# Routed attention with an ELU layer: row sums of two blocks in one set of matmuls, spread by GpSimd's transfers, and the first keys cut at 512

## The chip, the cores and the metric

The kernel runs on one core of one Trainium2 chip. The metric is device microseconds of one launch, the median of the runs shown. TensorE's granted clock is full in this execution (0.999 mean), so times of the two kernels can be compared line by line.

## The reference, cut to what matters

There are 4 batches (b), 8 heads, 768 tokens, head dimension 64 and 16 clusters; everything is fp32. A query may look at a key only where both are nearest to the same centroid of their head:

```
q_assign, k_assign = argmax over the 16 centroids of q_n . c_n and k_n . c_n
scores = q k^T / 8, and -1e9 where q_assign != k_assign
attn   = exp(scores - max); attn = attn / (sum(attn) + 1e-9)
x      = attn v                  # laid out as 3072 tokens x 512
out    = elu(x w_in) w_out       # w_in 512 x 2048, w_out 2048 x 512
```

## The kernel before

**Layout.** Scores are made transposed: keys on partitions, queries in the free dimension. One *block* is a batch, a half of the queries (`HS` = 384) and a pair of heads, so there are 32 blocks, 8 to a batch, counted n = 0 to 31. `at` = n mod 8 is the place in the batch. Keys come in six tiles of 128 (`kt`). The two heads of a pair are called e = 0 and 1.

**A slot** (`slot(n)`, about 10 us) is written out by hand (`manual_schedule`): every engine runs its instructions in the order of the text, and waits come from the data alone. On TensorE a slot is

- `row_sums(n - 2)` (L554): two matmuls of 64 ones by the 384 partial sums of head 0 and of head 1. They give the denominator of each query, already repeated on the 64 partitions of its head, in the PSUM bank `d_bank`;
- `values(n - 1)` (L536): twelve matmuls, probabilities times v, into `o_bank`;
- in the slots with `at` = 5, 6, 7 and one early slot of each batch (3 in the first, 1 later), `similar` (L427): four matmuls with 32 columns each, cluster scores for later queries or keys, into `d_bank`;
- six times `plain` (L498, q k^T) and `masked` (L511, adds the mask from one-hot cluster rows), into three banks used in turn (`ring`).

ScalarE runs `take_sums` (L563 Ln of the row sums, L564 a copy with its sum over the row, L565 Exp, together a first reciprocal), then `take_values` (L550, `o_bank` to `xT`), six exponentials (L520, into `p_out`), and the deferred list `later`, emptied by `flush` at the end of the slot: the copies of the one-hot rows (L456), the mask step for GpSimd (L463) and the conversion step of the weights (L330).

VectorE runs `sums_end` (L528 and L529: the six probability tiles added up, from 768 x 6 to 768), `divide` (L568, L569: one Newton step on the reciprocal), `assign` where the slot has one (L440, L442, L443, L453: the argmax), transposes of the next q and k (L659, L666, L673), the *weight steps* that `weigh` has planned, and `sums_begin` (L523). `divide` ends with one multiplication on GpSimd (L572) that scales the block of `xT`.

**Weight steps.** The weights arrive as 64-bit words and are turned to fp32 by `begin` (L320, L328 on VectorE, then L330 on ScalarE) and three `join`s (L340, L344, L350). `ROOM` gives each slot a credit, so what runs in which slot is fixed when the kernel is built.

**The start** (`slot_first`). The first q and k are turned by TensorE (`turned`, L577, copied out by ScalarE at L594) rather than VectorE, in halves of 384 keys: four pairs of heads, cluster scores of the first 384 keys, then the second half likewise. `assign` runs for the first q, the first and the second half of k. Then come the first six `plain`, `masked` and exponentials.

**After the attention** come the two matrix products with Strassen-like splits (L748, L994, L1066), fed by `w_step`, `elu_exp` and `elu`. The row sums of blocks 30 and 31 are done just ahead of the first product and inside its first unit (`finish_attention`). `findings` checks the row sums and the cluster counts on the chip; a general path runs only if that check fails.

**Buffers that the change names.** `summed`, `r_of`, `e_of` and `add_to` are parts of `sums_w`; `spare` holds weight words and later the products' temporaries. SyncE's queue issues nearly all transfers; GpSimd's own queue issues twelve stores of weight sums (L732) and two additions (L1390).

Of the kernel before, what the change touches and what calls it, by code (L numbers as in the profile page):

```python
# [19 lines left out]
P = 128  # L20
# [41 lines left out]
def main_path(ctx, tc, c, q, k, v, centroids, moe_w_in, moe_w_out, out):  # L62
# [71 lines left out]
    top = early[:, 7488:7512]  # L134
    hot_q = early[:, 7512:7896].bitcast(BF16).rearrange("p (s n) -> p s n", s=2)
# [3 lines left out]
    summed = sums_w[:, 4 * HS : 6 * HS]  # L139
# [111 lines left out]
    cT = const.tile([P, P], F32, name="cT")  # L251
    count = const.tile([P, 4 * B], F32, name="count")
    counted = 0
    r_sum = const.tile([P, len(blocks)], F32, name="r_sum")
    d_sum = const.tile([P, len(blocks)], F32, name="d_sum")
# [54 lines left out]
    def begin():  # L310

        nonlocal split
        if not wide:
            split += 1
            ask()
            return
        ask()
        w = words[split][0]
        to, e = like(pieces[split][0], w), like(ex_of, w)
        nc.vector.tensor_scalar(  # L320
            to.bitcast(U32),
            w[:, :, :, 1],
            0xFFFFF,
            1 << 20,
            op0=Alu.bitwise_and,
            op1=Alu.bitwise_or,
        )
        nc.vector.tensor_scalar(e, w[:, :, :, 1], 0x7FF00000, None, op0=Alu.bitwise_and)  # L328
        split += 1
        later.append(lambda: nc.scalar.activation(e, e, Act.Relu, scale=8.0, bias=off))  # L330
# [63 lines left out]
    credit, later = 0.0, []  # L394

    def flush():
        for other in later:
            other()
        later.clear()
# [25 lines left out]
    def similar(t, cols, ps):  # L425
        for pr in range(NPR):
            nc.tensor.matmul(  # L427
                ps[32 * pr : 32 * pr + 32, :HS],
                lhsT=cT[:, 32 * pr : 32 * pr + 32],
                rhs=t[pr][:, cols],  # L430
                start=True,
                stop=True,
            )

    def assign(hot, ps):


        nonlocal counted
        n = HS // NC
        nc.vector.transpose(sim, ps[:, :HS])  # L440
        s = sim.rearrange("p (n c) -> p n c", c=NC)
        nc.vector.tensor_reduce(top, s, axis=Axis.X, op=Alu.max)  # L442
        nc.vector.scalar_tensor_tensor(  # L443
            oh.rearrange("p (n c) -> p n c", c=NC),
            s,
            1.0,
            top.unsqueeze(2).to_broadcast([P, n, NC]),
            op0=Alu.mult,
            op1=Alu.is_equal,
            accum_out=count[:, counted : counted + 1],  # L450
        )
        counted += 1
        nc.vector.transpose(hot[:, 0], oh)  # L453
        for e in range(2):
            later.append(
                lambda e=e: nc.scalar.copy(  # L456
                    hot[64 * (1 - e) : 64 * (1 - e) + 64, 1], hot[64 * e : 64 * e + 64, 0]
                )
            )
# [12 lines left out]
    def clusters_k(b, half, ps):  # L472
        cols = ts(half, HS)
        similar(kT[b % 2], cols, ps)
        return lambda: assign(hot_k[b % 2][:, :, cols], ps)
# [11 lines left out]
    turn_of = 0  # L487
# [39 lines left out]
    def sums_end():  # L527
        nc.vector.tensor_tensor(add_to, add_to, probs_all[:, 8 * HS :], op=Alu.add)  # L528
        nc.vector.tensor_tensor(  # L529
            summed, add_to[:, : 2 * HS], add_to[:, 2 * HS :], op=Alu.add  # L530
# [21 lines left out]
    def row_sums(n):  # L552
        for e in range(2):
            nc.tensor.matmul(  # L554
                d_bank[64 * e : 64 * e + 64, :HS],
                lhsT=ones,
                rhs=summed[:, ts(e, HS)],
                start=True,
                stop=True,
            )  # L560

    def take_sums(n):
        nc.scalar.activation(r_of, d_bank[:, :HS], Act.Ln)  # L563
        nc.scalar.activation(e_of, d_bank[:, :HS], Act.Copy, accum_out=d_sum[:, n : n + 1])  # L564
        nc.scalar.activation(r_of, r_of, Act.Exp, scale=-1.0)  # L565

    def divide(n):
        nc.vector.tensor_tensor(e_of, e_of, r_of, op=Alu.mult)  # L568
        nc.vector.scalar_tensor_tensor(  # L569
            r_of, e_of, -2.0, r_of, op0=Alu.add, op1=Alu.mult, accum_out=r_sum[:, n : n + 1]  # L570
        )
        nc.gpsimd.tensor_tensor(x_of(n), x_of(n), r_of, op=Alu.mult)  # L572
# [8 lines left out]
    def turn(to, t, n):  # L581

        for i in range(HT):
            turned_by_pe(to[:, ts(i, P)], t, n + i)

    turns = 0

    def turned(to, t, n):
# [4 lines left out]
        turn(bank, t, n)  # L593
        nc.scalar.copy(to, bank[:, :HS])  # L594

    def slot_first():
# [10 lines left out]
        for pr in range(NPR):  # L607
            turned(kT[0][pr][:, :HS], first_k[pr], 0)
        told = [clusters_k(0, 0, o_bank)]
        flush()  # L610
        for pr in range(NPR):
            turned(kT[0][pr][:, HS:], first_k[pr], HT)
# [8 lines left out]
        for kt in range(NT):  # L621
            s = ring()
            plain(0, kt, s)
# [8 lines left out]
    def slot(n):  # L632
        b, at = n // NB, n % NB
        more = b + 1 < B
        if n > 1:
            row_sums(n - 2)
            take_sums(n - 2)
# [9 lines left out]
        if n > 0:  # L647
            sums_end()
        if n > 1:
            divide(n - 2)  # L650
# [24 lines left out]
        weigh(n)  # L675

# [7 lines left out]
        flush()  # L684
# [678 lines left out]
    def findings():  # L1363
# [6 lines left out]
        nc.vector.tensor_scalar(ok[:, 1:2], peak[:, 1:2], D_MAX, None, op0=Alu.is_lt)  # L1370
        nc.vector.tensor_scalar(same, count, float(HS // NC), None, op0=Alu.is_equal)
# [10 lines left out]
    last_n = len(blocks) - 1  # L1382
# [14 lines left out]
    row_sums(last_n - 1)  # L1397
    values(last_n)
    sums_end()
# [3 lines left out]
    take_sums(last_n - 1)  # L1403
    divide(last_n - 1)
    take_values(last_n)

    def finish_attention():
        row_sums(last_n)
        take_sums(last_n)
        divide(last_n)  # L1410
# [21 lines left out]
    for u in range(4):  # L1432
# [3 lines left out]
        if u == 1:  # L1436
            findings()
# [278 lines left out]
```

## Time and profile before

| what | value |
|---|---|
| median of 3 runs | 902.42 us (902.07 to 902.99) |
| the profiled execution: its time, its span | 902.24 us, 900.5 us |
| TensorE matmul busy | 889.9 us |
| VectorE busy | 725.9 us; 48.5 of each 50 us in the attention from 100 to 300 us |
| ScalarE, GpSimd busy | 449.5 us, 226.0 us |
| attention (to the first product at 341.6 us) | 38% of the span |
| row sums L554 | 32 times two matmuls, each of them two records: x128, 27.7 us busy |
| `divide` L568, L569 | 551 and 595 ns, x32 each |
| `take_sums` L563, L564, L565 | 480, 481 and 519 ns, x32 each |

Busy times are unions: matmuls in different columns of the array run at once, so 128 records of 512 ns make 27.7 us. A record's end is modelled, so distances in this document are taken from start to start.

### The profile page before, as it was taken

The page shows a single profiled execution, that of the slowest core. Times are in us where ns is not written, and L with a number is a line of the kernel's source. Part 1 is how long each engine was busy: PE and PEld are TensorE (multiplying, and loading weights), DVE is VectorE, ACT ScalarE, POOL GpSimd, SP SyncE. Part 2 cuts the span into 40 slices and gives each one's busy share as a digit, 9 for nine tenths or more (in the row PEclk, how much of TensorE's full clock was granted, in tenths as well). Part 3 has the DMA queues.
Part 4 walks back from the last instruction along what each step waited for, and adds up shares of the span by engine and source line. Part 5 has one row for each costly group of instructions (what it writes and reads, how often), then busy time and mean ns, then how long its engine had stood idle before and what let it go on. Part 6 is the DMA issues. An engine that isn't in the chain of part 4 may idle for free.

```text
span 900.5 us, 17050 instructions
## 1 busy us (share of the span) xinstructions
PE 889.9 (99%) x6473; PEld 687.6 (76%) x6473; DVE 725.9 (81%) x1067; ACT 449.5 (50%) x883; POOL 226.0 (25%) x257
## 2 busy tenths in 40 slices
PE   8999999999999999999999999999999999999997
PEld 4444444444444447899989999999999999999997
DVE  4699999999999997995389965895589558956885
ACT  5677787777776774420133225522552255225421
POOL 1022031221303244870033002520252025202300
PEclk9999999999999999999999999999999999999999
DMA  6765554365323622102698766176717761767272
GB/s 197 195 110 137 153 137 80 105 135 139 71 82 96 192 88 71 70 13 95 199 296 302 241 206 220 50 242 206 218 55 241 212 210 58 240 210 209 58 221 87
DMA packets 153209, 138.33 MB, mean 154 GB/s; under 512 B 89248, under 2 KB 106656, under 8 KB 152096
## 3 DMA queue, kind: packets, MB, share of 16 engines
q1 hardware_dynamic: 151584, 132.45, 50.2%
q0 software_dynamic: 1248, 4.20, 1.5%
q8 instruction: 53, 0.87, 0.4%
q10 hardware_dynamic: 288, 0.52, 0.2%
q14 instruction: 36, 0.29, 0.1%
HBM read 114.59 MB, written 21.50 MB: 151 GB/s over the span
## 4 chain that ended last, share of the span: by engine, by line
PE 92%; DVE 4%; DMA 2%; SPq 1%; issue 0%; ACT 0%; DVEq 0%
PE bank L994 23%; PE bank L748 16%; PE banks L498 12%; PE o_bank L536 12%; PE bank L1066 9%; PE o_bank L994 4%; PE o_bank L748 3%; PE banks L511 3%; PE d_bank L994 2%; PE d_bank L554 2%; PE o_bank L1066 2%; PE d_bank L427 1%; SPq L166 1%; DMA w_out<-in_k_dram 1%; PE d_bank L1066 1%; PE d_bank L748 1%
## 5 line engine op out<-in xcount | busy, mean ns | idle before, releaser
L520 ACT ACTIVATE p_out<-banks 128x768 f32<-128x768 f32 x192 | 155.2, 811 | 26.8 <-PE banks L511 25.4
L536 PE MATMUL o_bank<-p_out,kq_g 128*64 128x384 f32 x768 | 129.4, 486 | 0.1
L536 PEld LDWEIGHTS o_bank<-p_out,kq_g 128*64 128x64 f32 x768 | 55.0, 137 | 69.2 <-issue 62.7
L762 POOL TENSOR_SCALAR kq_g<-kq_g 128x512 f32<-128x512 f32 x96 | 67.8, 715 | 152.0 <-ACT kq_g L761 151.6
L572 POOL TENSOR_TENSOR xT<-xT,sums_w 128x384 f32<-128x384 f32 x32 | 35.3, 1103 | 222.0 <-DVE sums_w L569 164.6
L523 DVE TENSOR_TENSOR sums_w<-p_out 128x1536 f32<-128x1536 f32 x32 | 57.1, 1785 | 7.5 <-ACT p_out L520 7.5
L994 PE MATMUL bank<-w_out,kq_g 128*128 128x128 f32 x512 | 63.1, 275 | 0.0
L528 DVE TENSOR_TENSOR sums_w<-sums_w,p_out 128x1536 f32<-128x1536 f32 x32 | 59.0, 1845 | 3.3 <-DVE sums_w L523 0.5
L994 PEld LDWEIGHTS bank<-w_out,kq_g 128*128 128x128 f32 x512 | 60.5, 192 | 0.5
L761 ACT ACTIVATE kq_g<-bank 128x512 f32<-128x512 f32 x68 | 39.8, 602 | 38.9 <-PE bank L748 17.3
L748 PE MATMUL bank<-xT,spare 128*128 128x256 f32 x256 | 59.2, 379 | 0.0
L748 PEld LDWEIGHTS bank<-xT,spare 128*128 128x128 f32 x256 | 48.3, 190 | 6.4
L748 PE MATMUL bank<-x_sum,w_in 128*128 128x256 f32 x224 | 52.9, 379 | 0.0
L765 DVE SCALAR_TENSOR_TENSOR kq_g<-kq_g,bank 128x512 f32<-128x512 f32 x68 | 44.9, 680 | 6.2 <-POOL kq_g L762 6.2
L748 PEld LDWEIGHTS bank<-x_sum,w_in 128*128 128x128 f32 x224 | 42.6, 190 | 5.8
L1280 DVE TENSOR_TENSOR kq_g<-kq_g 128x1024 f32<-128x1024 f32 x36 | 45.2, 1263 | 1.5 <-PE bank L994 1.5
L1084 POOL TENSOR_TENSOR spare<-x_sum 128x128 f32<-128x128 f32 x16 | 7.3, 455 | 154.4 <-PE bank L1066 88.8
L463 POOL TENSOR_SCALAR kq_g<-w_out,big,minus 128x768 bf16<-128x768 bf16 x16 | 34.1, 2138 | 46.8 <-ACT w_out L456 46.8
L550 ACT ACTIVATE xT<-o_bank 128x384 f32<-128x384 f32 x32 | 15.7, 490 | 48.3 <-PE o_bank L536 48.3
L498 PE MATMUL banks<-x_sum,xT 64*128 64x384 f32 x192 | 39.8, 492 | 0.0
L498 PE MATMUL banks<-x_sum,kq_g 64*128 64x384 f32 x192 | 39.6, 491 | 0.0
L498 PE MATMUL banks<-kq_g 64*128 64x384 f32 x192 | 39.6, 491 | 0.0
(326 smaller groups left out, 2030.2 us busy)
## 6 DMA issues: line engine op xcount, KB each, us to landing
kq_g<-in_v_dram SPq DMA_DIRECT2D x32, 384.0 KB, 3.6
sums_w<-far_s_s SPq DMA_DIRECT2D x42, 256.0 KB, 3.7
spare<-w_far SPq DMA_DIRECT2D x32, 256.0 KB, 3.1
words_w<-far_s_s SPq DMA_DIRECT2D x26, 256.0 KB, 3.5
out_dram<-p_out SPq DMA_DIRECT2D x22, 256.0 KB, 3.4
w_out<-in_q_dram SPq DMA_DIRECT2D x112, 48.0 KB, 2.7
sums_w<-far_s_q SPq DMA_DIRECT2D x21, 256.0 KB, 3.6
words_w<-far_a_s SPq DMA_DIRECT2D x20, 256.0 KB, 3.7
```

What stands on the lines that cost most here:

```text
L498: nc.tensor.matmul(s[:, e, :HS], lhsT=kT[b % 2][pr][rows, ts(kt, P)], rhs=qT[half][pr][rows], start=True, stop=False,)
L520: nc.scalar.activation(probs[kt], s[:, :, :HS], Act.Exp, scale=SCALE)
L523: nc.vector.tensor_tensor(add_to, probs_all[:, : 4 * HS], probs_all[:, 4 * HS : 8 * HS], op=Alu.add)
L528: nc.vector.tensor_tensor(add_to, add_to, probs_all[:, 8 * HS :], op=Alu.add)
L536: nc.tensor.matmul(o_bank[64 * e : 64 * e + 64, :HS], lhsT=v_raw[n % 2][:, e, kt], rhs=probs[kt][:, e], start=(kt == 0), stop=(kt == NT - 1),)
L748: nc.tensor.matmul(bank[:, ts(f, QS)], lhsT=left[:, ch, ts(f, P)], rhs=right[:, ch], start=first and f == 0 and ch == 0, stop=ch == 1, ski ...
L761: nc.scalar.activation(to, as_part(bank, to), Act.Exp)
L762: nc.gpsimd.tensor_scalar(to, to, 1.0, 0.0, op0=Alu.min, op1=Alu.max)
L765: nc.vector.scalar_tensor_tensor(to, to, -1.0, as_part(bank, to), op0=Alu.add, op1=Alu.max)
L994: nc.tensor.matmul(bank[:, :P], lhsT=left[:, f], rhs=right[:, f], start=first and f == 0, stop=last and f == 3, skip_group_check=True,)
L1066: nc.tensor.matmul(bank[:, ts(f, P)], lhsT=left[:, ts(f, P)], rhs=right, start=m in ("m1", "m5") and f == 0, stop=True, skip_group_check=True,
L1280: nc.vector.tensor_tensor(b[to][:, f], b[x][:, f], b[y][:, f], op=op)
```

## The change

1. **Row sums.** They are done in odd slots only, for the two blocks n - 3 and n - 2 at once. Four matmuls of 32 ones (`ones[:, :32]`) fill the four 32-row strips of `d_bank`: block n - 3 head 0, head 1, block n - 2 head 0, head 1. The last two blocks follow in the first unit of the product. `summed` becomes two buffers; the new one lies in `spare`.
2. **Their reciprocals.** `take_sums` and the Newton step run once for a pair of blocks, on 128 partitions. `reciprocals` goes to a place in `xT` (or `add_to`) that is not yet in use. It comes behind the weight steps on VectorE; before, `divide` stood ahead of `assign`, the transposes and the weight steps.
3. **The spread.** Each sum now stands on 32 partitions where 64 are wanted. Two transfers issued by GpSimd copy 64 rows twice each into `r_of` and `e_of` (128 x 384 fp32, 192 KB each). In the next slot `scale_x` multiplies the two blocks on GpSimd.
4. **ScalarE's conversion step** L330 goes on a list of its own (`powers`), emptied in the next slot behind `take_sums`; before, it was ahead of it.
5. **The first k** is cut in 512 and 256 keys. Pair 0's last 256 are turned ahead of the cluster scores of the first part, and the first `plain` goes ahead of the second cluster scores. The counts that `findings` compares are corrected for the sizes.

```diff
+    CUT = 512
+    told_in = {
+        HS: (sim, oh, top),
+        CUT: (p_out[:, :512], p_out[:, 512:768].bitcast(BF16), p_out[:, 768:800]),
+        S - CUT: (sim[:, :256], oh[:, :256], top[:, :16]),
+    }
...
-    summed = sums_w[:, 4 * HS : 6 * HS]
+    summed = [spare.rearrange("p a n -> p (a n)")[:, 2048 : 2048 + 2 * HS]]
+    summed.append(sums_w[:, 4 * HS : 6 * HS])
...
-        later.append(lambda: nc.scalar.activation(e, e, Act.Relu, scale=8.0, bias=off))
+        powers.append(lambda: nc.scalar.activation(e, e, Act.Relu, scale=8.0, bias=off))
...
     def row_sums(n):
-        for e in range(2):
+
+        for at in range(0, P, 32):
+            j, e = at // 64, at // 32 % 2
             nc.tensor.matmul(
-                d_bank[64 * e : 64 * e + 64, :HS],
-                lhsT=ones,
-                rhs=summed[:, ts(e, HS)],
+                d_bank[at : at + 32, :HS],
+                lhsT=ones[:, :32],
+                rhs=summed[(n - 1 + j) % 2][:, ts(e, HS)],
...
-    def divide(n):
+    def reciprocals(n):
+        at = n // 2
         nc.vector.tensor_tensor(e_of, e_of, r_of, op=Alu.mult)
         nc.vector.scalar_tensor_tensor(
-            r_of, e_of, -2.0, r_of, op0=Alu.add, op1=Alu.mult, accum_out=r_sum[:, n : n + 1]
+            to_spread(n),
+            e_of,
+            -2.0,
+            r_of,
+            op0=Alu.add,
+            op1=Alu.mult,
+            accum_out=r_sum[:, at : at + 1],
         )
-        nc.gpsimd.tensor_tensor(x_of(n), x_of(n), r_of, op=Alu.mult)
+
+    def to_spread(n):
+
+        if n == last_n:
+            return add_to[:, :HS]
+        return x_of(last_n - NB if n < last_n - NB else last_n)
+
+    def scale_x(n, r):
+        nc.gpsimd.tensor_tensor(x_of(n), x_of(n), r, op=Alu.mult)
+
+    def spread(n):
+        r = to_spread(n)
+        for j, to in enumerate((r_of, e_of)):
+            nc.gpsimd.dma_start(
+                to, r[64 * j : 64 * j + 64].unsqueeze(1).to_broadcast([64, 2, HS])
+            )
...
         for pr in range(NPR):
-            turned(kT[0][pr][:, :HS], first_k[pr], 0)
+            turned(kT[0][pr][:, :CUT], first_k[pr], 0)
+        turned(kT[0][0][:, CUT:], first_k[0], CUT // P)
         told = [clusters_k(0, 0, o_bank)]
         flush()
-        for pr in range(NPR):
-            turned(kT[0][pr][:, HS:], first_k[pr], HT)
+        for pr in range(1, NPR):
+            turned(kT[0][pr][:, CUT:], first_k[pr], CUT // P)
+        first = ring()
+        plain(0, 0, first)
         told.append(clusters_k(0, 1, d_bank))
...
     def slot(n):
...
-        if n > 1:
-            row_sums(n - 2)
-            take_sums(n - 2)
+        sums_of = n - 2 if n > 1 and n % 2 else None
+        pair_done = n - 4 if n >= 4 and n % 2 == 0 else None
+        if sums_of is not None:
+            row_sums(sums_of)
+            take_sums(sums_of)
+        flush(powers)
...
         if n > 0:
-            sums_end()
-        if n > 1:
-            divide(n - 2)
+            sums_end(n - 1)
+        if pair_done is not None:
+            scale_x(n - 4, r_of)
+            scale_x(n - 3, e_of)
...
         weigh(n)
+        if sums_of is not None:
+            reciprocals(sums_of)
+            spread(sums_of)
...
-    row_sums(last_n - 1)
     values(last_n)
-    sums_end()
+    sums_end(last_n)
...
-    take_sums(last_n - 1)
-    divide(last_n - 1)
+    scale_x(last_n - 3, r_of)
+    scale_x(last_n - 2, e_of)
     take_values(last_n)
 
     def finish_attention():
         row_sums(last_n)
         take_sums(last_n)
-        divide(last_n)
+        reciprocals(last_n)
+        spread(last_n)
...
         run(unit(0, u, finish_attention if u == 0 else None, fill_weights))
         if u == 1:
+            scale_x(last_n - 1, r_of)
+            scale_x(last_n, e_of)
             findings()
```

## The prediction

> **What bounds the kernel now.** I read the page's first four parts, then the groups by line and shape up to 360 us, then the timeline of a slot in the middle. First the busy times, the slices and the shares of the chain that ended last.
>
> ```profile
> PE 889.9 (99%) x6473; PEld 687.6 (76%) x6473; DVE 725.9 (81%) x1067; ACT 449.5 (50%) x883; POOL 226.0 (25%) x257
> ...
> PE   8999999999999999999999999999999999999997
> ...
> PE 92%; DVE 4%; DMA 2%; SPq 1%; issue 0%; ACT 0%; DVEq 0%
> ```
>
> TensorE (PE) is busy in nearly every slice and holds 92% of the chain. So an instruction taken from TensorE is worth its distance to the next one, if no other engine comes to the front. VectorE (DVE) is close behind it in the attention, at 48.5 of 50 us; it is the one to watch. Now one slot, TensorE's timeline from 150 to 172 us (start, length, engine, line, operation, tiles):
>
> ```profile
> 155.21 0.87 PE L554 MATMUL d_bank<-sums_w,ones 128*64 128x384 f32 x4
> 155.90 4.04 PE L536 MATMUL o_bank<-p_out,kq_g 128*64 128x384 f32 x24
> 159.87 0.85 PE L427 MATMUL d_bank<-xT,cT 128*32 128x384 f32 x8
> 160.65 0.92 PE L498 MATMUL banks<-kq_g 64*128 64x384 f32 x4
> ...
> 165.70 0.87 PE L554 MATMUL d_bank<-sums_w,ones 128*64 128x384 f32 x4
> ```
>
> From start to start: a row sum takes 155.90 - 155.21 = 0.69 us, values 3.97, cluster scores 160.65 - 159.87 = 0.78, the scores 5.05. The slot has 10.49 us and no gap. The row sum runs two matmuls of 64 columns at once, the cluster scores four of 32 columns. The four cost 0.09 us more than the two, not twice as much. That is the number on which most of this forecast stands.
>
> The one gap of TensorE in the middle of the attention is at 252 us; from that stretch of the timeline, all engines (in brackets: idle time before, and what ended it):
>
> ```profile
> 250.13 1.15 ACT L330 ACTIVATE sums_w<-sums_w,off 128x1024 uint32<-128x1024 uint32 x1 [1.28 <-DVE sums_w L328]
> 251.19 0.47 ACT L563 ACTIVATE sums_w<-d_bank 128x384 f32<-128x384 f32 x1
> 251.56 0.48 ACT L564 ACTIVATE sums_w<-d_bank 128x384 f32<-128x384 f32 x1
> ...
> 252.18 0.85 PE L427 MATMUL d_bank<-kq_g,cT 128*32 128x384 f32 x8 [0.92 <-ACT sums_w L564]
> ```
>
> VectorE was late with L328; ScalarE's L330 waited for it; the row sums' readers L563 and L564 stood behind L330; and the cluster scores waited for their bank. And the start, same view:
>
> ```profile
> 19.74 2.42 ACT L520 ACTIVATE p_out<-banks 128x768 f32<-128x768 f32 x3 [0.87 <-PE banks L511]
> 22.75 0.33 PE L511 MATMUL banks<-kq_g,w_out 64*128 64x384 bf16 x1 [0.64 <-ACT w_out L456]
> 24.63 4.09 PE L536 MATMUL o_bank<-p_out,kq_g 128*64 128x384 f32 x24
> ```
>
> The first exponential starts at 19.74. The fourth key tile (keys 384 to 511) then waits 0.64 us for the one-hot rows of the second half; slot 1 begins at 24.63.
>
> **What the Trainium skill says.** *TensorE: Matmul & The Clock Gate*, Part 3: matmuls whose outputs lie in different 32-partition strips of PSUM run at once. The trace agrees: 0.78 us for four strips here. *DMA: Bandwidth & Descriptors*, "Anatomy of one DMA": a transfer issued by GpSimd takes about 2.0 us plus its bytes / 436e3; for 196,608 bytes that gives an estimate of 2.0 + 0.45 = 2.45 us. The trace has stores of 256 KB from the same queue, from the source view of L732 (min/median/max):
>
> ```profile
> L732 POOL DMA_DIRECT2D w_far<-spare x8: 569/576/598, 318.3 to 386.2; - x8
> ...
> DMA to landing us min/median/max: 2.3/2.4/5.8
> ```
>
> So 0.58 us of GpSimd for the issue and 2.4 us to landing. *GPSIMD Engine Reference*, the table of facts at its head: its SBUF interfaces are shared with VectorE, with contention for instructions of two SBUF inputs. The trace agrees: L528 takes 1.76 us alone and 2.27 beside the mask step L463 (at 240.49).
>
> **The change part by part.**
>
> 1. *Row sums on TensorE.* Before: 32 times 0.69 = 22.1 us (slots 2 to 31, one behind the last slot, one in the first unit), all in a gapless stream. After: 16 times. The form (128 rows, 32 columns, 384 wide, four at once) is that of L427, so 0.78, or 12.5 us. Gain 9.6 us. Bounds: 0.69 for the four (11.1, gain 11.0), or 1.0 if the switches of shape on both sides cost more (16.0, gain 6.1).
>
> 2. *Their reciprocals.* ScalarE loses 16 x (480 + 481 + 203 + 519 ns) = 26.9 us, VectorE 16 x (551 + 595 + 82 ns) = 19.6 us. Neither is counted as gain; what matters is whether they keep pace. A pair of plain slots shortens from 19.4 to 19.4 - 2 x 0.69 + 0.78 = 18.8 us; VectorE's share of it, 97% or 18.8 us, falls by 1.23 to 17.6. It gains slack, 0.6 us a pair.
>
> 3. *Newton step behind the weight steps.* `assign`, the transposes and L328 come 1.15 us earlier in odd slots and have no step ahead of them in even ones. The row sums wait for nothing that got later. Behind the step on VectorE there is only `sums_begin`, and whatever of the queue comes after, at the time it has now. The step waits for ScalarE's L565, some 3 us into the slot, and it starts 8 us or more into it: no wait.
>
> 4. *The spread.* Two issues on GpSimd, 2 x 0.58, wait for the Newton step. Queued behind them are the mask steps L463 and, a slot on, two `scale_x` of 1.0 us. The longest chain, with `at` = 5 (counted from the start of the next, even slot): Newton step done at about 1.7 (where L523 starts now, at 156.88 against 155.21), issues to 2.9, masks 4.65 to 7.6 (transfers landed by 5.3), two `scale_x` to 9.6. The even slot with cluster scores lasts 10.49 - 0.69 = 9.8, and ScalarE is free for the next Ln, which overwrites `r_of`, only about 1.0 later. Cover 1.2 us. Beyond that ScalarE itself has about 2 us: `take_sums` lasts 1.7, so it would end at 2.7, and `take_values` behind it waits for TensorE until 0.78 + 3.97 = 4.75. Without masks: 1.9 + 1.2 + 2.4 + 2.0 = 7.5 of 9.0. The masks come at most 1 us later; the pair made in slot 3 is needed soonest, 4.7 us into slot 4. It starts when the one-hot copies end, 2.1 into the slot (56.26 against 54.18), its first half takes 1.9, and the issues are over by then. Cost 0; if the cover of 0.7 fails there, up to 1 us once. SyncE's queue keeps its order. The transfers add 6.3 MB to an attention with half of its transfer time free.
>
> 5. *L330 behind `take_sums`.* The stall of 0.92 us at 252 loses its cause: nothing but the row sums stands ahead of L563. Late next is L550 behind L330, in the same slot; it starts 4 us into the slot, after VectorE's L328 even at its latest. Gain 0.9; bounds 0 and 0.9.
>
> 6. *The first k.* Turning 512 keys of the last pair takes 16 records for 12 (48 take 2.84 us at 14.42, so +0.24), its copy is wider (+0.1) and so is the last matmul (+0.2): the first cluster scores end at about 15.0, 14.49 now. VectorE's four steps of `assign` grow by 512/384 from 2.4 to about 3.1 us: done at 18.1. The first one-hot copy (0.51 now, 0.65 then) ends at 18.8, the second at 19.4, with `plain` long done; `masked` starts between these, against 19.37 now. From there to the values are five tiles at 0.81 and 0.33: 18.8 + 4.38 = 23.2, or 23.8. Keys 384 to 511 are in the first part, so the wait of 0.64 goes; the last two tiles' rows are ready at about 22.3 against 22.0 to 22.6 wanted. Slot 1 at 23.2 to 23.8 against 24.63: gain 0.8 to 1.4, I take 1.2, as the first tile needs the first copy alone; bounds 0 (the longer first `assign` eats it) and 1.6.
>
> 7. *In the first units of the product* `findings` has two small VectorE steps more (0.16 us each, off the chain), and GpSimd has two issues (1.2 us) where it had one multiplication (1.0), and two multiplications after unit 1, where it sits idle 2.3 us ahead of L762 at 360. TensorE has no gap there now. 0.
>
> Sum: 9.6 + 0.9 + 1.2 = 11.7 us off the profiled 902.24 (span 900.5 and 1.7 around it), 890.5. The median of the runs is 0.2 above that execution: **890.7**. By the bounds alone, 6.1 to 13.5 less, or 889 to 896.5.
>
> **Rivals.**
>
> - *VectorE becomes the bound.* For: 97% busy, up to 2.8 us behind at 250 us. Against: it loses more than TensorE does, and the first exponential of a slot waits for L523, which is done 1.5 us or more before. If half of the row-sum gain went so: 895.5.
> - *The strips don't overlap here,* because all four read `ones` and two different buffers. Then the four cost 1.4 us, as two pairs would: row-sum gain zero, 900.3. Against: L427 also has four sources.
> - *Slower: the spread lands late.* `r_of` is overwritten by ScalarE's Ln two slots on, and `take_values` and six exponentials are queued behind it. Without masks the chain of step 4 ends at 5.1 us plus the landing time L, and the Ln wants it at 10.0 and can lose 2.0 more: TensorE pays L - 6.9 per pair. The gain of 11.7 over 15 pairs is 0.8, so it decides from L = 7.7 us. The two additions L1390, from the same queue, land in 10.8 and 13.6 us; with 10.8, 15 x 3.9 = 58 us, 949. Against: they move four times a spread's bytes or more and add; L732 lands in 2.4, at most 5.8.
> - *The change doesn't do what it says:* wrong counts would send it down the general path, which does all of the work again: by the 341.6 us of the attention alone, over 1,240. The sums are 32 - 8 and 16 + 8, both the 24 wanted.
>
> **How the numbers follow.** Forecast 0.82; VectorE's bound 0.08; no overlap 0.04; late spread 0.05; general path 0.01. A measurement of this kernel can tell about 0.2%, or 1.8 us, from none. Faster holds the forecast, VectorE's case and half of the third (900.3 is at the edge): 0.92; same 0.02; slower 0.06. The range, 887.5 to 897, takes in the bounds and VectorE's case.
>
> **What would show it.** Right: L554 with 32 columns at x128, 0.78 us from start to start; plain slots of 9.02 and 9.8 us in turn; no gap at 252; slot 1 before 23.9; L550's idle time mostly PE's. Wrong: gaps before L498 or L427 ended by ScalarE, ScalarE's L563 waiting for POOL, landings over 7 us, or L536 waiting for DVE.

## The result, and the profile after

The changed kernel takes 910.48 us (median of 4 runs, 909.96 to 911.1), the kernel before 902.27 beside it: ratio 1.009, interval 1.0072 to 1.0107. It is 0.9% slower; forecast were 890.7 us and a range up to 897. The profiled execution took 910.05 us with a span of 908.3.

From the page of the changed kernel, the busy times, TensorE's slices and granted clock, and the shares of the chain:

```profile
PE 886.4 (98%) x6470; PEld 682.3 (75%) x6473; DVE 721.0 (79%) x1021; ACT 426.3 (47%) x819; POOL 237.4 (26%) x289
...
PE   8999999999979899999999999999999999999997
...
PEclk9999999999989999999999999999999999999999
...
PE 71%; DVE 15%; DMA 4%; issue 4%; SPq 3%; POOL 2%; ACT 1%; DVEq 0%; ACTq 0%; POOLq 0%
```

TensorE has less to do, as intended. But it is no longer busy in every slice: there is a 7 from 250 to 272 us, with the granted clock at 8, and an 8 from 295 to 318 us. And its share of the chain fell from 92% to 71%; VectorE's rose to 15%.

TensorE's timeline of two undisturbed slots shows that the part planned for it came true:

```profile
134.43 4.09 PE L550 MATMUL o_bank<-p_out,kq_g 128*64 128x384 f32 x24
138.45 0.92 PE L512 MATMUL banks<-kq_g 64*128 64x384 f32 x4
...
143.50 0.52 PE L570 MATMUL d_bank<-spare,ones 128*32 128x384 f32 x2
...
144.28 4.09 PE L550 MATMUL o_bank<-p_out,kq_g 128*64 128x384 f32 x24
148.30 0.85 PE L437 MATMUL d_bank<-x_sum,cT 128*32 128x384 f32 x8
...
154.13 2.16 PE L550 MATMUL o_bank<-p_out,kq_g 128*64 128x384 f32 x12
```

The row sums (now L570) of two blocks take 144.28 - 143.50 = 0.78 us. From the values of one slot to those of the next it is 9.85 us with them or with cluster scores, 9.07 with neither and 10.63 with both. What is longer than this is called a *stall* here and is counted to the earlier of the two slots (some recorded expectations count it to the later one; 0.05 us and less is left out). The changed kernel has these: slots 6 and 8, 0.15 each; slot 10, 2.68; slot 16, 0.33; slot 18, 2.21; slot 22, 0.32; slot 24, 8.36; slot 27, 2.68 us: 16.9 in all. The kernel before has one of 0.99, in slot 23, and one of 0.22.

The books close on that. Slot 1's values start 0.73 us earlier (23.90 against 24.63). From there to the values of block 31 it is 319.86 us against 312.55, 7.3 more. Without its stalls it would be 303.0, 9.6 less than before, near the sum that was forecast. What follows costs 1.2 more. Together 7.8, which is 910.05 - 902.24.

TensorE's longest waits, from the view of waits (waiting instruction <- what ended it: total, times, longest):

```profile
PE banks L512 <- ACT p_out L534: 5.2, 1, 5.2
PE d_bank L570 <- DVE sums_w L543: 3.0, 2, 1.9
PE o_bank L550 <- DMA kq_g<-in_v_dram: 2.6, 1, 2.6
```

There is one line for each of three causes.

**A, slot 24.** The timeline of all engines around 266 us:

```profile
259.32 0.56 DVE L587 SCALAR_TENSOR_TENSOR xT<-sums_w 128x384 f32<-128x384 f32 x1
...
260.46 1.21 POOL L609 DMA_DIRECT2D sums_w<-xT  x2 [14.52 <-DVE xT L587]
...
266.92 0.49 ACT L564 ACTIVATE xT<-o_bank 128x384 f32<-128x384 f32 x1 [8.68 <-DMA sums_w<-xT]
...
268.17 1.65 PE L512 MATMUL banks<-x_sum,kq_g 64*128 64x384 f32 x4 [5.19 <-ACT p_out L534]
```

`to_spread(21)` is the place of block 23 in `xT`. The reciprocals of blocks 20 and 21 are made late in slot 23 and are read from there by the transfers L609. In slot 24 `take_values(23)` (L564) writes its block into that very place, so it waits for the transfers' read. They were issued at 260.46, behind the Newton step L587, and landed some 6 us later. ScalarE stood 8.68 us, six exponentials behind it. TensorE then stood 5.19 us, and its next four matmuls took 1.65 us instead of 0.81: it ran at half speed until about 274 (granted clock 0.50 from 268 to 274), which makes up the rest of the 8.36. The Trainium skill says this in *TensorE: Matmul & The Clock Gate*, Part 1: after an idle window of about 3.4 us the clock returns to half rate. The trace agrees.

**B, slots 10 and 18.** The same view around 118 us:

```profile
113.78 1.03 ACT L468 COPY w_out<-w_out 64x384 bf16<-64x384 bf16 x2
...
115.99 0.56 DVE L587 SCALAR_TENSOR_TENSOR xT<-sums_w 128x384 f32<-128x384 f32 x1
...
117.13 1.19 POOL L609 DMA_DIRECT2D sums_w<-xT  x2 [11.99 <-ACT sums_w L339]
...
118.25 2.04 POOL L475 TENSOR_SCALAR kq_g<-w_out,big,minus 128x768 bf16<-128x768 bf16 x2
...
118.33 4.54 DVE L542 TENSOR_TENSOR sums_w<-sums_w,p_out 128x1536 f32<-128x1536 f32 x1
...
120.17 3.56 POOL L604 TENSOR_TENSOR xT<-xT,sums_w 128x384 f32<-128x384 f32 x2
...
124.59 0.84 PE L570 MATMUL d_bank<-sums_w,ones 128*32 128x384 f32 x4 [1.85 <-DVE sums_w L543]
```

L542 adds the last two of the six probability tiles to their sum; it is called the *halving* here, as in the recorded expectations. It takes 1.76 us when it is alone. Here it takes 4.54, and the row sums wait for L543 behind it. It starts 0.08 us behind the masks L475 on GpSimd. Taken one by one, the two masks last 1.09 and 1.07 us and the first multiplication L604 1.08, each its usual time; the second multiplication, which starts last, lasts 2.45. So the halving seems to have stood through three GpSimd instructions (118.33 to about 121.1), then ran its 1.76, and the fourth stood behind it. The Trainium skill, *SBUF — State Buffer*, "Who interferes with whom", says it so: "Issue order, not op shape, decides who blocks." The trace agrees in slot 10, but slot 18 shows that the starts on record don't settle the order to a tenth of a microsecond:

```profile
200.04 0.57 POOL L609 DMA_DIRECT2D sums_w<-xT  x1 [0.21 <-issue]
200.45 3.75 DVE L542 TENSOR_TENSOR sums_w<-sums_w,p_out 128x1536 f32<-128x1536 f32 x1
200.63 1.96 POOL L475 TENSOR_SCALAR kq_g<-w_out,big,minus 128x768 bf16<-128x768 bf16 x2
```

Here the halving has the earlier start by 0.18 us, with the second issue still running, and the masks go ahead of it all the same. In slot 26, where the masks start 0.52 us behind it, it keeps its 1.76 us and the masks pay.

The same place in the kernel before (L463 is the mask, L528 the halving):

```profile
116.98 1.78 DVE L523 TENSOR_TENSOR sums_w<-p_out 128x1536 f32<-128x1536 f32 x1
117.66 4.42 POOL L463 TENSOR_SCALAR kq_g<-w_out,big,minus 128x768 bf16<-128x768 bf16 x2 [4.14 <-ACT w_out L456]
118.86 2.35 DVE L528 TENSOR_TENSOR sums_w<-sums_w,p_out 128x1536 f32<-128x1536 f32 x1
```

Here the masks start inside L523 and pay themselves: 4.42 us for two, and the halving loses only 0.6. In the changed kernel the issue L609 stands ahead of the masks. Their rows are ready at 114.81, when the copies L468 end, but the issue waits for the Newton step L587. It starts 0.58 us behind the end of that step, takes 1.2 us, and so lets the masks go just as L537 (L523 before) ends and L542 begins, 3.4 us after their rows were ready. (The bracket behind L609 names ScalarE, the last event that the profile saw; the distance of 0.58 us from the end of L587 is the same in slot 24, where L587 is named.)

**C, slot 27.** The queue of SyncE and GpSimd:

```profile
286.48 5.86 POOL L475 TENSOR_SCALAR kq_g<-w_out,big,minus 128x768 bf16<-128x768 bf16 x2 [0.54 <-issue]
...
292.29 1.86 POOL L1440 DMA_DIRECT2D w_in<-w_in  x2
292.37 0.37 SPq L309 DMA_DIRECT2D w_out<-in_moe_w_out_dram  x1
...
292.84 0.41 SPq L190 DMA_DIRECT2D kq_g<-in_v_dram  x1
...
305.93 1.51 PE L550 MATMUL o_bank<-p_out,kq_g 128*64 128x384 f32 x8 [2.62 <-DMA kq_g<-in_v_dram]
```

A request for weights (L309) takes a place that the masks read. The two masks of slot 26, which started 0.52 us behind the halving, took 5.86 us; so the request waited, and the load of v (L190) stood behind it in SyncE's queue. It went out at 292.84, beside the two adding transfers L1440, and landed 13.0 us later (3.0 at best, 4.6 in the middle); the values waited 2.62. In the kernel before the same load has the same neighbours. It went out at 284.90 and landed in 10.5 us, but that was 3.0 us before its values began at 298.33.

### The profile page after: what moved, and what is told of

It is laid out like the page before. It is cut to its first block, busy times and chain, and to the rows that moved or that the text cites. A ratio compares the mean times of both kernels' runs of the same rounds, so it can differ in the third digit from the quotient of the medians.

```text
span 908.3 us, 17043 instructions
## 1 busy us (share of the span) xinstructions
PE 886.4 (98%) x6470; PEld 682.3 (75%) x6473; DVE 721.0 (79%) x1021; ACT 426.3 (47%) x819; POOL 237.4 (26%) x289
## 4 chain that ended last, share of the span: by engine, by line
PE 71%; DVE 15%; DMA 4%; issue 4%; SPq 3%; POOL 2%; ACT 1%; DVEq 0%; ACTq 0%; POOLq 0%
PE bank L1041 23%; PE bank L795 11%; PE bank L1113 9%; PE o_bank L550 7%; PE banks L512 6%; PE o_bank L1041 4%; DVE sums_w L542 3%; PE d_bank L1041 2%; PE o_bank L795 2%; DVE sums_w L537 2%; DMA kq_g<-in_v_dram 2%; SPq L174 2%; PE o_bank L1113 2%; PE banks L525 2%; DVE sums_w L349 1%
## 5 line engine op out<-in xcount | busy, mean ns | idle before, releaser
L534 ACT ACTIVATE p_out<-banks 128x768 f32<-128x768 f32 x192 | 152.4, 812 | 33.2 <-PE banks L525 22.3
L550 PEld LDWEIGHTS o_bank<-p_out,kq_g 128*64 128x64 f32 x768 | 52.3, 137 | 77.8 <-issue 71.6
L609 POOL DMA_DIRECT2D sums_w<-xT x30 | 18.2, 629 | 213.5 <-DVE xT L587 75.1
L542 DVE TENSOR_TENSOR sums_w<-sums_w,p_out 128x1536 f32<-128x1536 f32 x32 | 69.3, 2167 | 4.2 <-ACT p_out L534 1.4
L537 DVE TENSOR_TENSOR sums_w<-p_out 128x1536 f32<-128x1536 f32 x32 | 59.2, 1851 | 16.5 <-ACT p_out L534 16.4
L604 POOL TENSOR_TENSOR xT<-xT,sums_w 128x384 f32<-128x384 f32 x32 | 44.4, 1421 | 30.6 <-DMA sums_w<-xT 30.5
L512 PE MATMUL banks<-x_sum,kq_g 64*128 64x384 f32 x192 | 41.9, 516 | 5.2 <-ACT p_out L534 5.2
L564 ACT ACTIVATE xT<-o_bank 128x384 f32<-128x384 f32 x32 | 15.7, 490 | 65.4 <-PE o_bank L550 56.5
```

Of the source, the lines that this page charges most:

```text
L512: nc.tensor.matmul(s[:, e, :HS], lhsT=kT[b % 2][pr][rows, ts(kt, P)], rhs=qT[half][pr][rows], start=True, stop=False,)
L534: nc.scalar.activation(probs[kt], s[:, :, :HS], Act.Exp, scale=SCALE)
L537: nc.vector.tensor_tensor(add_to, probs_all[:, : 4 * HS], probs_all[:, 4 * HS : 8 * HS], op=Alu.add)
L550: nc.tensor.matmul(o_bank[64 * e : 64 * e + 64, :HS], lhsT=v_raw[n % 2][:, e, kt], rhs=probs[kt][:, e], start=(kt == 0), stop=(kt == NT - 1),)
L604: nc.gpsimd.tensor_tensor(x_of(n), x_of(n), r, op=Alu.mult)
```

## Experiments

Each was timed beside the kernel before on the same chip (901.45 to 901.64 us in these sets). *The theory*: the gain on TensorE is real, and it is lost to the place that the spread reads (A), to masks and multiplications that start ahead of VectorE's halving (B), and to the late request (C). *Rivals*: VectorE's load as such; the transfers' landing; other parts of the change.

| kernel | median us | ratio to before, interval | stalls, us | halving, mask, mean ns |
|---|---|---|---|---|
| before | | 1 | 1.2 | 1845, 2276 |
| changed | 910.48 | 1.0090 [1.0072, 1.0107] | 16.9 | 2167, 1337 |
| no_spread_no_scale | 892.38 | 0.9893 [0.9876, 0.9909] | 0 | 1866, 2351 |
| scratch | 901.16 | 0.9991 [0.9980, 1.0002] | 7.4 | 2335, 1072 |
| scratch_no_scale | 895.46 | 0.9926 [0.9909, 0.9942] | 4.3 | 2041, 1564 |
| scratch_step_first | 896.27 | 0.9941 [0.9924, 0.9958] | 3.9 | 2027, 2291 |
| step_first | 897.09 | 0.9955 [0.9938, 0.9971] | 3.8 | |
| ask_later | 908.38 | 1.0083 [1.0066, 1.0100] | 12.0 | |
| first_k_alone | 901.37 | 0.9998 [0.9989, 1.0006] | 1.0 | |
| conversion_later_alone | 900.73 | 0.9990 [0.9981, 0.9999] | 0 | |
| scratch_spread_after_mask | 903.48 | 1.0023 [1.0013, 1.0032] | 12.3 | 2026, 2232 |
| scratch_step_first_ask_later | 897.75 | 0.9958 [0.9944, 0.9972] | 3.3 | |
| best_less_room | 893.92 | 0.9917 [0.9901, 0.9934] | 0.2 | 2036, 2192 |
| less_room_alone | 900.14 | 0.9987 [0.9979, 0.9995] | 4.4 | 2320, 1070 |

Stalls and means come from the one profiled execution of each; the masks of the start are left out of their mean.

**no_spread_no_scale: is the gain on TensorE there at all?**

```diff
     def scale_x(n, r):
-        nc.gpsimd.tensor_tensor(x_of(n), x_of(n), r, op=Alu.mult)
+        return
     def spread(n):
+        return
```

> The changed kernel without the spread's transfers and without the multiplications of xT on GpSimd; the rows of x stay unscaled. Theory A (what the change costs comes from GpSimd: its work beside VectorE's two-input additions, and the waits for its transfers): all stalls of slots 11, 19, 25 and 28 go, L542 falls from 2.17 to 1.85 us or less, about 891 as was forecast. Rival C (VectorE's own work bounds the shorter slots, with or without GpSimd): the stalls of slots 11 and 19 stay, 897 to 900.

892.38 us and no stall. From the values of slot 1 to those of block 31 it takes 302.98 us, 9.57 less than before. This kernel leaves out work that the result needs, so it is a bound and not a version. It shows that all the rest of the change is worth its price, and that the loss lies with the transfers and the multiplications.

**scratch: a place of its own for the spread of slot 23 (A).**

```diff
     def to_spread(n):
+        if n == last_n - NB - 2:
+            return raw_k[1][:, :HS]
```

> The changed kernel with one place altered: in slot 23 the reciprocals go to an idle part of w_out's early area instead of the place of block 23 in xT. Theory A (ScalarE's take_values of block 23 waits 8.7 us for the transfers that read that place, and TensorE then loses 8.4 us in slot 25): slot 25 falls back to about 9.85 us, L564 no longer waits for a transfer, 7 to 9 us less than the changed kernel, 902 to 904. Rival B (the transfers or VectorE are late anyway and another wait takes its place): 2 us less or none, 908 to 910.

901.16, some 9 us less than the changed kernel and no different from the kernel before. The stall of slot 24 is gone. Slots 10 and 18 keep theirs (2.63 and 2.97), so A and B are two things. The groups of this kernel show who pays in B: the masks run at their best, the halving does not (mean of one after the bar):

```profile
L542 DVE TENSOR_TENSOR sums_w<-sums_w,p_out 128x1536 f32<-128x1536 f32 x32 | 74.7, 2335 | 2.9
...
L475 POOL TENSOR_SCALAR kq_g<-w_out,big,minus 128x768 bf16<-128x768 bf16 x14 | 14.2, 1072 | 0.0
```

**scratch_no_scale: the same without the multiplications.**

```diff
     def scale_x(n, r):
-        nc.gpsimd.tensor_tensor(x_of(n), x_of(n), r, op=Alu.mult)
+        return
```

> As scratch, and without the multiplications of xT on GpSimd (rows of x stay unscaled); the spread's transfers stay. Theory A1 (the multiplications are what slows VectorE's L542): L542 back to 1.85 us, 892 to 895. Rival A2 (the mask steps L475, held back by the issue of the transfers to the start of L542, are what slows it): L542 stays at 3.6 us in slots 4, 6, 14, 22, mean about 2.05, 897 to 901.

895.46, which lies between the two forecasts. The halving still takes 3.5 to 3.8 us in the four slots that A2 names, and its mean of 2041 ns is A2's. But in slots 10 and 18, which had the stalls, it takes 2.60 us and comes in ahead of the second mask, here in slot 10:

```profile
115.84 3.56 POOL L475 TENSOR_SCALAR kq_g<-w_out,big,minus 128x768 bf16<-128x768 bf16 x2
115.95 2.60 DVE L542 TENSOR_TENSOR sums_w<-sums_w,p_out 128x1536 f32<-128x1536 f32 x1
```

These two slots have no stall. So the multiplications have a part in B beside the masks. Why the halving came in there and not in slots 14 and 22, where the masks have the same lead of 0.1 us, is not shown. What stalls are left are in slots 27 and 28, where the two masks of slot 26 took 5.87 us and loads of v were late: cause C, without A.

**scratch_step_first: the Newton step and the issue directly behind VectorE's last sum.**

```diff
             sums_end(n - 1)
+        if sums_of is not None:
+            reciprocals(sums_of)
+            spread(sums_of)
...
         weigh(n)
-        if sums_of is not None:
-            reciprocals(sums_of)
-            spread(sums_of)
```

> As scratch, with the Newton step and the spread put back ahead of assign, transposes and weight steps, where divide stood. Theory A (GpSimd's steps fall on L542 because the transfers are issued at the end of VectorE's list): L542 back to about 1.85 us, no wait of L570 for VectorE in slots 11 and 19, 891 to 896. Rival C (VectorE has too much to do in any order): within 2 us of scratch.

896.27, just above its forecast. The halving's mean is 2.03 us where 1.85 was expected. The issue is long over when the masks become ready; they start inside L537 again and pay, as the groups show,

```profile
L542 DVE TENSOR_TENSOR sums_w<-sums_w,p_out 128x1536 f32<-128x1536 f32 x32 | 64.9, 2027 | 2.9
...
L475 POOL TENSOR_SCALAR kq_g<-w_out,big,minus 128x768 bf16<-128x768 bf16 x14 | 32.0, 2291 | 25.3 <-ACT w_out L468 25.3
```

and as slot 10 does, beside the 4.54 of the changed kernel:

```profile
114.17 1.75 DVE L537 TENSOR_TENSOR sums_w<-p_out 128x1536 f32<-128x1536 f32 x1
114.21 5.02 POOL L475 TENSOR_SCALAR kq_g<-w_out,big,minus 128x768 bf16<-128x768 bf16 x2 [2.88 <-ACT w_out L468]
...
116.03 2.35 DVE L542 TENSOR_TENSOR sums_w<-sums_w,p_out 128x1536 f32<-128x1536 f32 x1
```

The stall of slot 10 is gone, that of slot 18 is 1.00. The same instructions are issued as in scratch, in another order; that is worth some 5 us.

**step_first: the order alone, with the place as changed.** The diff of scratch_step_first without that of scratch.

> The changed kernel with the Newton step and the spread put back ahead of assign, transposes and weight steps; the place of the reciprocals stays as changed. Theory A (the wait of L564 in slot 24 and the slow L542 both come from issuing the transfers at the end of VectorE's list): the transfers of slot 23 land before take_values wants the place, so no wait in slot 24 even without another place, and L542 about 2.0 us; 895 to 898. Rival D (the place alone is the fault in slot 24): slot 24 still waits several us, 901 to 905.

897.09, within the interval of scratch_step_first. With the spread this early L564 does not wait for the transfers in slot 24; what it waits for is TensorE's values:

```profile
251.76 1.20 POOL L609 DMA_DIRECT2D sums_w<-xT  x2 [9.59 <-DVE w_out L452]
...
256.04 0.49 ACT L564 ACTIVATE xT<-o_bank 128x384 f32<-128x384 f32 x1 [1.49 <-PE o_bank L550]
```

The stall of 0.80 that slot 24 keeps comes from exponentials that waited for VectorE's L537, and scratch_step_first has it too (1.61). So A is not the place alone: it needs the late issue too. Either repair removes it; of these two, only the order removes B.

**scratch_spread_after_mask: a test of B by itself.** The issue goes behind the masks; the Newton step stays last.

```diff
             reciprocals(sums_of)
-            spread(sums_of)
...
+        if sums_of is not None:
+            spread(sums_of)
```

> Nothing of the computation is left out. The kernel is scratch (the spread of slot 21's reciprocals has a place of its own), with one thing moved: GpSimd issues the two transfers behind the slot's two masks instead of ahead of them; the Newton step stays last on VectorE. Theory (the issue, which waits for the Newton step, holds the masks until they start together with VectorE's two-input halving, which then runs at 3.6 to 4.5 us): with the masks free to start earlier, that halving falls to about 2.4 us in the slots with masks, its mean to about 2.0 us (scratch 2.34), the stalls of slots 10 and 18 shrink to under 1 us each, and the time is 896 to 899 us. Rival (the place of the issue does not matter, it is the multiplications' two-input work that loads VectorE): mean halving stays above 2.2 us, time 900 to 902 us.

The halving fell as B said, from 2335 to 2026 ns, the masks rose from 1072 to 2232, and the stalls of slots 10 and 18 fell to 0.62 and 0.77. The time did not follow: 903.48 us. The transfers now start later still, and the prediction's slower rival appeared, in slot 19:

```profile
209.10 3.71 POOL L606 TENSOR_TENSOR xT<-xT,sums_w 128x384 f32<-128x384 f32 x2 [5.87 <-DMA sums_w<-xT]
...
211.17 0.49 ACT L580 ACTIVATE sums_w<-d_bank 128x384 f32<-128x384 f32 x1 [5.29 <-POOL xT L606]
...
216.13 1.65 PE L512 MATMUL banks<-x_sum,xT 64*128 64x384 f32 x4 [3.73 <-ACT p_out L534]
```

GpSimd's multiplications (here L606) wait 5.87 us for the transfers, ScalarE's Ln (L580), which overwrites what they read, 5.29 us for them, TensorE 3.73 and then at half speed again: a stall of 6.5. Slot 5 has a smaller one of 2.0 by the same waits. My expectation of 896 to 899 was wrong because I looked at the meeting of masks and halving and not at the landing.

**ask_later: the request of slot 27 a slot later (C).**

```diff
-            places.append((early[:, 6144:].unsqueeze(1), into + 6))
-            ask()
...
+        elif n == 3 * NB + 2:
+            places.append((early[:, 6144:].unsqueeze(1), into + 6))
+            ask()
```

> The changed kernel with one request for weights (SyncE's L309 behind slot 25, which waits for the mask steps) moved behind slot 26, so that it isn't ahead of the load of v for block 27. Theory E (slot 27's wait of 2.7 us for v comes from SyncE standing at that request): this wait goes, 906 to 908.5, the rest as in the changed kernel. Rival F (the load is late because the two additions L1440 fill the DMA engines): v still lands 10 us or more after its issue and the wait stays above 1.5 us, 909 to 911.

The load of v went out at 286.31, 3.8 us ahead of the adding transfers, and landed in 3.0 us; slot 27 has no stall. So the wait came from the request. That a load beside the adding transfers lands late, which is rival F's point, is not touched by this. The time, 1.0083, can't be told from the changed kernel's 1.009: the intervals overlap.

**first_k_alone and conversion_later_alone: parts 5 and 4 of the change, each on the kernel before.**

```diff
-            turned(kT[0][pr][:, :HS], first_k[pr], 0)
+            turned(kT[0][pr][:, :CUT], first_k[pr], 0)
...
```

> The kernel before with the first k cut in 512 and 256 alone (with the corrected counts). Forecast: slot 1 starts 0.8 to 1.4 us earlier than 24.63 and the kernel takes 0.8 to 1.4 us less. Rival G (VectorE's longer first assign eats it): slot 1 earlier by 0.5 us or less.

```diff
-        later.append(lambda: nc.scalar.activation(e, e, Act.Relu, scale=8.0, bias=off))
+        powers.append(lambda: nc.scalar.activation(e, e, Act.Relu, scale=8.0, bias=off))
```

> The kernel before with L330 moved behind the take_sums of the next slot alone. Forecast: the gap of 0.92 us before L427 in slot 23 goes and nothing else moves, 0.9 us less. Rival H (ScalarE gets the wait somewhere else, L550 or the exponentials): less than 0.3 us.

The first moves slot 1 from 24.63 to 23.96 in its profile, but 0.9998 with an interval of 0.0017 does not show that 0.7 in the total. The second takes the stall of slot 23 away and gives 0.9990, about the 0.9 us forecast. Neither loses anything, so neither explains the slower time.

**scratch_step_first_ask_later and best_less_room: all repairs, and then VectorE's load.** The first has the three edits above together. The second has in addition

```diff
-        + [2.3, 2.6, 3.0, 3.0, 1.4, 1.7, 2.6, 2.6] * (B - 2)
+        + [2.1, 2.3, 2.7, 2.7, 1.2, 1.5, 2.3, 2.3] * (B - 2)
```

> Nothing of the computation is left out. The kernel as changed with all three repairs: a place of its own for the spread of slot 21, the reciprocals and the issue of the spread directly behind VectorE's last sum, and the request for the second product's weights a slot later. The step-first version with its own place measured 896.3 us, and lost nothing in slot 27. Theory: the request only mattered where a mask came late; so the same time within 0.7 us, 895.5 to 897. Rival: the request also delays other loads of late slots: 893 to 895.

> Nothing of the computation is left out. The kernel of scratch_step_first_ask_later with the planner's allowance for weight steps in the middle slots cut by some tenth, so that a few weight steps move from VectorE's list in attention to behind it. Theory (what is left of the loss, about 4 us in four late slots, is VectorE's lateness beside the two-input work of GpSimd): the stalls shrink, attention ends 1 to 3 us earlier, 893 to 895.5 us. Rival: the moved weight steps then hold the second product's first weights: no gain, 896 us or more.

897.75 (forecast 895.5 to 897) and 893.92. With the order right, the request is worth nothing measurable. The remaining stalls (0.60, 1.03 and 1.65 us in slots 16, 18 and 24) were VectorE's lateness: a few weight steps less, and 0.2 us of stalls are left. best_less_room beats both kernels, 0.8% under the one before. (The lighter list on the kernel before was not timed; that kernel has 1.2 us of stalls to lose.) Its chain is TensorE's again:

```profile
PE 92%; DVE 3%; issue 2%; POOL 1%; DMA 0%; ACT 0%; SPq 0%; POOLq 0%; DVEq 0%; ACTq 0%
```

**less_room_alone: load or order?** The lighter list on the changed kernel, without its repairs.

> Nothing of the computation is left out. The changed kernel with one thing else: the planner's allowance for weight steps in the slots of the two middle batches cut by some tenth, as in best_less_room, and none of its three repairs. The loss of the changed kernel has two readings. Load: VectorE simply has too much to do in a slot, and the order only decides who notices; then a lighter list also brings the Newton step forward in time, ScalarE's wait in slot 24 shrinks to under 3 us, and the time is 893 to 897 us. Order: the Newton step at the end of the list and the place that is read late cost what they cost whatever the load, since the issue still holds the masks until they meet the two-input halving (3.6 us or more in five or more slots); then part of the loss stays, 898 to 906 us. I expect the second, about 901, as the wait of 8.7 us in slot 24 is larger than the lightening of VectorE's list.

900.14. The lighter list takes some 9 us off the changed kernel, since the Newton step, last in the list, comes earlier (2.5 us into slot 24 and not 3.6): the stall of slot 24 is 2.4, though ScalarE still waits 5.57 us there. The halving stays at 2320 ns, and takes 3.57 and 3.75 us in slots 10 and 18; but the stalls there are 0 and 0.36. So a slow halving need not cost TensorE anything: that depends on how full VectorE's list is. Load and order each explain a part; the same list with the three repairs is 6 us faster.

## Why the prediction was wrong, step by step

1. *Row sums on TensorE:* right. 0.78 us for the four, no stall from the strips. The slot's rest is 9.07 us, not 9.02, since the values take 4.02 us from start to start where they took 3.97; over 31 slots that is 1.6 us. In the stretch of the attention steps 1 and 5 promised some 10.5; 9.57 came where nothing was in the way.

2. *The reciprocals' load:* the fall of 1.23 us a pair is right, and the conclusion "It gains slack" is not. The busy times from 100 to 300 us, VectorE third, for the kernel before, no_spread_no_scale and scratch_step_first:

```profile
100.00:300.00 200.00, 199.08 (x1342) 92.75 (x1342) 193.79 (x225) 151.76 (x245) 46.24 (x32) 1.00 0.49 119
```

```profile
100.00:300.00 200.00, 200.00 (x1384) 91.03 (x1382) 187.79 (x197) 142.54 (x213) 32.24 (x18) 1.00 0.49 122
```

```profile
100.00:300.00 200.00, 198.16 (x1360) 89.65 (x1358) 194.62 (x195) 138.99 (x209) 74.58 (x53) 1.00 0.55 138
```

Per pair of slots (20.16, 19.55 and 19.80 us) VectorE is busy 19.5, 18.4 and 19.3 us. So 1.2 us are freed where no multiplications and transfers stand beside VectorE. With them, even in the good order, 0.3 are left; L353, 1.22 us elsewhere, takes 2.02 beside a multiplication in slot 10 of scratch_step_first. My sum gave all of the 1.2 to slack and left out that GpSimd's work now comes in the same slot for two blocks.

3. *Newton step last:* "The row sums wait for nothing that got later" looked at the wrong reader. What waits for the step is the issue of the spread, and behind it on GpSimd the masks.

4. *The spread, "Cost 0":* this is the step that failed, in three terms.
   - A reader that I left out. I followed `r_of`, the transfers' destination, and not the place that they read. `take_values(23)` overwrites that place one slot later: 8.4 of the 16.9 us.
   - A delay that I did see, but took too small and priced at nothing. I put the end of the Newton step 1.7 to 1.9 us into the even slot. In slots 6 to 24 it came 2.1 to 4.1 us into it (3.7 in slot 10, 4.0 in slot 18), and at most 2.2 in no_spread_no_scale; the issue begins 0.58 us later still. So "The masks come at most 1 us later" is wrong: in slots 6, 10, 14, 18 and 22 the masks stood 2.3 to 4.0 us behind the issue with their rows ready, and 0.1 in the kernel before. This moves their start from inside L537 to the start of L542, which changes who blocks whom: 5.2 us in slots 10, 18 and 22, where TensorE waits for what follows the slow halving. I had read 1.76 against 2.27 us in the kernel before as the size of this contention. It was the size with GpSimd as the loser.
   - The landing. I took 2.45 us from *DMA: Bandwidth & Descriptors* and 2.4 from the stores L732. The source view of L609 has

```profile
DMA to landing us min/median/max: 2.6/3.9/6.8
```

   The measurement decides: beside the loads of an attention slot the price is half as much again, and the cover of 1.2 us was gone in the middle case already. It stayed under the 7.7 us of the slower rival, so that rival did not decide the changed kernel; its waits did make the stalls of slots 5 and 19 in scratch_spread_after_mask.

   The wait C, 2.7 us, belongs to the same step, but not to the masks' wait behind the issue: in slot 26 they started as soon as their rows were ready (286.31, and 286.48), lost to VectorE and took 5.86 us, where they took 4.10 before. I wrote of SyncE's queue that it "keeps its order". It does; that is why the load of v stood behind the request.

5. *L339 (L330 before) behind `take_sums`:* right, 0.9990 of the kernel before and no gap.

6. *The first k:* 0.7 us in these two profiles instead of 1.2, within the bounds. Single profiles differ by more: over the twelve kernels with this cut slot 1 starts at 23.28 to 24.19 (mean 23.8), in the two without it at 24.63 and 24.78. In the changed kernel's profile a term that I missed is again VectorE beside GpSimd:

```profile
15.60 1.96 POOL L475 TENSOR_SCALAR kq_g<-w_out,big,minus 128x768 bf16<-128x768 bf16 x2 [14.24 <-ACT w_out L468]
...
16.77 1.33 DVE L455 SCALAR_TENSOR_TENSOR p_out<-p_out 128x512 bf16<-128x512 f32 x1
...
18.90 0.33 PE L525 MATMUL banks<-kq_g,w_out 64*128 64x384 bf16 x1 [0.77 <-DVE w_out L465]
```

   The first `assign` ran from 15.29 to 18.85, 3.6 us and not 3.1, as L455 took 1.33 us beside a mask (0.56 for 384 columns in later slots), and the first masked tile waited 0.77 for it.

7. *The first product:* not told apart from 0. From the last values to the end it is 1.2 us more in the changed kernel, 0.5 in scratch and no_spread_no_scale, and 1.8 in best_less_room, which moves weight steps there. But it is 1.1 more in conversion_later_alone too, which has none of this step's changes, so single profiles differ by as much.

Of the rivals, "VectorE becomes the bound" had its mechanism partly right: VectorE's lateness is what made the Newton step late, and what best_less_room removed. No rival held A or B, so the chance of 0.06 for slower rested on a mechanism that was not the one.

## What to carry to other kernels

For a transfer between buffers list four parties, not two: who writes its source next, who reads its destination, what waits behind its issue on the issuing engine, and what waits behind that. Where GpSimd and VectorE meet, ask which of the two starts first, because a shift of some tenths of a microsecond in that order can move the bill from the engine with slack to the one without: in the changed kernel the masks went ahead when they started 0.18 us behind the halving and paid at 0.52. When TensorE's slots get shorter, ask too which engine keeps its old pace, because what waits for that engine comes later in the slot. A step that others wait for belongs at the head of the list of a nearly full engine; with that order, a lighter list and the other two repairs this change gains 0.8% instead of losing 0.9%.

## What was not expected of the hardware

- A VectorE instruction that meets several GpSimd instructions in a row can stand through more than one of them: L542 by its length through three in slot 10 (2.8 us before its own 1.76). It is not always so. In the kernel before, and in slots 10 and 18 of scratch_no_scale, it came in behind the first mask. What decides this is not shown.
- The times of some kernels vary more from run to run than those of the kernel before (900.7 to 903.1 us in 23 runs): 898.2 to 903.9 us in less_room_alone and 900.7 to 908.2 in scratch_spread_after_mask (20 runs each). The cause was not tested.
- Loads of v that start beside the two adding transfers land late: in 13.0 us in the changed kernel and 10.5 in the kernel before, against 3.0 in ask_later for the same load 3.8 us ahead of them.
